# Attention and gated long convolution on one core: another order of the loads, two gate projections of batch 0 ahead of batch 1's k^T v, and two more output buffers at the end

## The chip, the core and the metric

The kernel runs on one core of a Trainium2 chip. The metric is device time in microseconds (us). Before the change the median of three runs is 268.35 us (268.27 to 268.37).

## What is computed

Linear attention without a softmax, normalised per head, feeds a gated convolution over the sequence. Cut to what matters, with B = 8 batches, H = 8 heads, S = 576 positions, D = 64, and 512 channels:

```python
kv  = einsum('bhsd,bhse->bhde', k, v)
o   = einsum('bhsd,bhde->bhse', q, kv)
x   = o / sqrt(mean(o * o, -1) + 1e-6) * g_norm      # then heads side by side: (B, S, 512)
x1, x2, x3 = split(x @ w_proj, 3, axis=-1)
c   = irfft(rfft(x2, axis=1) * rfft(filter_fft, axis=0), n=S, axis=1)
out = (x1 * c * x3) @ w_out
```

Inputs and output are float32.

## The kernel before, in words

**Layout.** Channels lie on the partitions, four tiles of 128 channels (NDC), with the 576 positions in the free dimension. All eight batches are unrolled. For each batch the stages are: `kv` (line 195), k^T v per head, 40 small matmuls (line 204) that accumulate over five chunks of the sequence, four full ones and a tail of 64 rows padded with zeros, and a copy into the diagonal blocks of `kvblk` (line 208); `qtr` (line 210), q transposed by TensorE (line 219) and copied by VectorE (line 222); `att_o`, `att_r`, `att_x` (lines 226 to 261), q times k^T v, its square (line 234), the sum of squares by a matmul with 0/1 blocks (line 250), log and exp for 1/sqrt (lines 251 and 254), and x; `fold` (line 263), which adds and subtracts thirds of the sequence so that the transform becomes three smaller ones; `proj2` (lines 326, 330, 338), the projection x2 that the filter is applied to, on the folded x; `fft` (line 342), the forward transform as matmuls (lines 353, 360), multiplied with the filter's transform on VectorE (lines 355, 356, 361) and summed on GpSimd (line 357); `proj13` (line 363), for one channel tile the projections x1 (copied by ScalarE, line 376) and x3 (multiplied with x1 by VectorE, line 378), sixteen matmuls on line 372; `invc` and `inv`, the inverse transform and the gate; `outp`, the product with w_out and the store. The last batch has a combined end, `last` (line 441), with five output copies (lines 470 and 472), each followed by two stores (line 475), one on SP's queue and one on ScalarE's.

**Once per call.** The cosine and sine tables are made on VectorE and ScalarE (lines 136 to 151) and transposed (`tables`, line 180). The filter is loaded by eight DMAs on SP's queue (`load_filter`, line 115), 1920 KB in all, folded by VectorE (`fold_filter`, line 282) and transformed by TensorE (`gen_h`, line 298).

**Loads.** q, k, v and the weights are cast from float32 to bfloat16 by their DMAs, all on GpSimd's queue: per batch two for k, two for v (`load_kv`, line 81) and two for q (`load_q`, line 89), into two sets of buffers. Their order at the start is k, v, q of batch 0, the parts 1, 0, 2 of w_proj (w2, w1, w3), w_out, and k, v, q of batch 1. At most eight of these transfers are under way: the ninth waits for the first, and so on. GpSimd's queue is in order, and GpSimd's sums of line 357 stand in it too.

**Order of the work.** The kernel is written in a framework that plans each engine's order at build time. Among the instructions whose operands the plan takes as ready, it takes the one that stands first in the program; so an instruction can be put ahead of earlier ones that the plan holds to be waiting. `tc.keep_in_program_order(ins)` pins an instruction behind the one that stands just before it in the program on the same engine. On the chip every engine then runs its planned order and waits on semaphores. PSUM is used as four buffers of two banks (tag `ps`), the output tiles have three buffers (tag `ot`), and the products of `fft` and the two filter tiles `fa` and `fc` share two larger ones (tag `tpw`). The program order before is `kv(0)`, `qtr(0)`, the filter loads, `tables`, the attention of batch 0, `zeros(1)` (the zero rows of batch 1's tails and of its `kvblk`), `fold_filter`, and then for every batch `proj2(b)`, `kv(b + 1)`, `qtr(b + 1)`, for batch 0 `gen_h`, the loads of batch b + 2, and a loop over channel tiles with `fft`, `att_o(b + 1)`, `proj13(b)` and the rest of the attention of b + 1.

Of the kernel before, what the change touches and what calls it, by code (L numbers as in the profile page):

```python
# [9 lines left out]
FP32 = mybir.dt.float32  # L10
# [10 lines left out]
def kernel(  # L21
# [59 lines left out]
    def load_kv(b):  # L81
        for i, src in enumerate((k, v)):
            nc.gpsimd.dma_start(  # L83
                out=kvm[b % 2][i].rearrange("p h c d -> p h (c d)"),
                in_=bass.AP(tensor=src.tensor, offset=src.offset + b * H * S * D,
                            ap=[[4 * D, P], [S * D, H], [1, 4 * D]]))
            nc.gpsimd.dma_start(out=kvt[b % 2][i][:TAIL], in_=src[b, :, 4 * P:S, :].transpose([1, 0, 2]))

    def load_q(b):
        for g in range(2):  # L90
            nc.gpsimd.dma_start(
                out=qb[b % 2][64 * g:64 * g + 64].rearrange("p h (m x) -> p (h m) x", m=3),
                in_=bass.AP(tensor=q.tensor, offset=q.offset + (b * H + 4 * g) * S * D,
                            ap=[[3 * D, 64], [SB * D, 12], [1, 3 * D]]))

    load_kv(0)
    load_q(0)

    wo = consts.tile([P, NDC, DM], BF16)
    wp = consts.tile([P, NDC, D3], BF16)  # L100
# [1 line left out]
    def load_w(dst, src):  # L102
        nc.gpsimd.dma_start(out=dst, in_=src.rearrange("(c p) d -> p c d", p=P))

    for part in (1, 0, 2):
        load_w(wp[:, :, part * DM:(part + 1) * DM], moe_w_proj[:, part * DM:(part + 1) * DM])
    load_w(wo, moe_w_out)
    load_kv(1)
    load_q(1)


    fa = work.tile([P, 4, DM], FP32, name="fa", tag="tpw", bufs=2)
# [2 lines left out]
    def load_filter():  # L115

        for t in (fa, fc):
            tc.keep_in_program_order(nc.vector.memset(t[:, :, 0:1], 0.0))
        f4 = moe_filter_fft.rearrange("(m p c) d -> c p m d", m=3, c=3)
        lo, hi = slice(0, 64), slice(64, 128)  # L120
        for o, i in ((fa[lo, 0:3], f4[0]), (fa[hi, 0:3], f4[1]), (fa[lo, 3], f4[2][:, 1]), (fc[lo, 0], f4[2][:, 0]),
                     (fc[lo, 1], f4[2][:, 2]), (fc[hi, 0:2], f4[0][:, 1:3]), (fc[lo, 2:4], f4[1][:, 1:3]),
                     (fc[hi, 2:4], f4[2][:, 1:3])):
            nc.sync.dma_start(out=o, in_=i)
# [44 lines left out]
    def zeros(i):  # L169
        for t in kvt[i]:  # L170
            tc.keep_in_program_order(nc.vector.memset(t[TAIL:P], 0.0))
        tc.keep_in_program_order(nc.vector.memset(kvblk[i], 0.0))
# [21 lines left out]

    def kv(b):
        (km, vm), (kt, vt) = kvm[b % 2], kvt[b % 2]
        st[b] = {}
        kvp = ps_tile("ps_kv")
        for j in range(NDC):
            for c in range(NSC):  # L200
                for hp in range(2):
                    h = 2 * j + hp
                    kk, vv = (km[:, h, c], vm[:, h, c]) if c < 4 else (kt[:, h], vt[:, h])
                    nc.tensor.matmul(kvp[64 * hp:64 * hp + 64, 0, j * D:(j + 1) * D], kk, vv,  # L204
                                     start=(c == 0), stop=(c == NSC - 1))
        for h in range(2):
            r = slice(64 * h, 64 * h + 64)
            nc.scalar.copy(out=kvblk[b % 2][r, :, r], in_=kvp[r, 0, 0:4 * D].rearrange("p (j e) -> p j e", j=4))

    def qtr(b):  # L210

        qT = work.tile([P, NDC, NR, 64], BF16, name="qT", tag="qT")
        st[b]['qT'] = qT.rearrange("p j c t -> p j (c t)")
        for jj in range(2):
            tp = psp.tile([P, 2, 1024], BF16, name="ps_qT", tag="ps")
            for bank, cs in ((0, range(0, 4)), (1, range(4, NR))):
                for i, c in enumerate(cs):
                    for hp in range(2):
                        nc.tensor.transpose(tp[64 * hp:64 * hp + 64, bank, i * P:(i + 1) * P],  # L219
                                            qb[b % 2][:, 2 * jj + hp, c * D:(c + 1) * D], ident)  # L220
                n = len(cs)
                nc.vector.tensor_copy(  # L222
                    out=qT[:, 2 * jj:2 * jj + 2, cs[0]:cs[0] + n].rearrange("p g c t -> p c g t"),
                    in_=tp[:, bank, 0:n * P].rearrange("p (c g t) -> p c g t", c=n, g=2))
# [57 lines left out]
    def fold_filter():  # L282
        ff = hst['ff'] = work.tile([P, NSC, DM], BF16, name="ff", tag="ff")
        tc.keep_in_program_order(nc.vector.memset(ff[64:P, 1], 0.0))
        t0 = work.tile([P, 2, DM], FP32, name="t0", tag="ot", bufs=3)
        nc.vector.tensor_add(out=t0[:, 0], in0=fa[:, 0], in1=fa[:, 1])
        nc.vector.tensor_add(out=ff[:, 0], in0=t0[:, 0], in1=fa[:, 2])
        nc.vector.tensor_add(out=t0[0:64, 1], in0=fc[0:64, 0], in1=fc[0:64, 1])
        nc.vector.tensor_add(out=ff[0:64, 1], in0=t0[0:64, 1], in1=fa[0:64, 3])
        nc.vector.tensor_sub(out=ff[:, 2], in0=fa[:, 0], in1=fa[:, 2])  # L290
        fc2 = fc.rearrange("p (a b) d -> p a b d", a=2)
        nc.vector.tensor_sub(out=ff[:, 3:5], in0=fc2[:, :, 0], in1=fc2[:, :, 1])
        asc = hst['asc'] = consts.tile([P, 2], FP32, name="asc")
        tc.keep_in_program_order(nc.vector.memset(asc, 2.0 / S))
        tc.keep_in_program_order(nc.vector.memset(asc[0:1, 0:1], 1.0 / S))
        tc.keep_in_program_order(nc.vector.memset(asc[96:97, 0:1], 1.0 / S))
# [144 lines left out]
    def last(b):  # L441

        Y, g13 = st[b]['Y'], st[b]['g13']
        yg = work.tile([P, NDC, S], BF16, name="yg", tag="yg", bufs=3)
        po = [ps_tile("ps_out") for _ in range(3)]

        def part(dc):
            kw = dict(start=(dc == 0), stop=(dc == NDC - 1))
            for c in range(4):
                nc.tensor.matmul(po[c // 2][:, c % 2], yg[:, dc, c * P:(c + 1) * P], wo[:, dc], **kw)  # L450
            for i, y in enumerate((yt[0], yg)):
                nc.tensor.matmul(po[2][64 * i:64 * i + 64, 0], y[:, dc, 4 * P:S], wo[:, dc], **kw)

        for dc in range(NDC):
            ip = ps_tile("ps_inv")
            for g in range(6):
                n = N1 if g < 2 else P
                for h in range(2):
                    nc.tensor.matmul(ip[:, h, 0:TH], Y[:n, g, dc * P:(dc + 1) * P], IV[:n, g, h * TH:(h + 1) * TH],  # L459
                                     start=(g == 0), stop=(g == 5))  # L460
            nc.vector.tensor_mul(out=yg[:, dc].rearrange("p (a b) -> p a b", a=2), in0=ip[:, :, 0:TH],
                                 in1=g13[:, dc].rearrange("p (a b) -> p a b", a=2))
            if dc:
                part(dc - 1)
        part(NDC - 1)
        for c in range(NSC):
            ot = work.tile([P, 2, DM], FP32, name="ot", tag="ot", bufs=3)
            src = po[c // 2][:, c % 2]
            if c % 2:
                nc.vector.tensor_copy(out=ot[:, 0], in_=src)  # L470
            else:
                nc.scalar.copy(out=ot[:, 0], in_=src)
            for i in range(2):
                bb, blk = (b, 2 * c + i) if c < 4 else (b - 1 + i, NR - 1)
                (nc.scalar if i else nc.sync).dma_start(out=o_rows(bb, blk), in_=ot[64 * i:64 * i + 64, 0])


    kv(0)
    qtr(0)
    load_filter()  # L480
    tables()
    for j in range(NDC):
        att_o(0, j)
        if j:
# [4 lines left out]
    att_r(0, NDC - 1)  # L489
    att_x(0, 1)  # L490
    fold(0, 1)
    zeros(1)
    fold_filter()
    for b in range(B):
        nxt = b + 1 < B
        proj2(b)
        if nxt:
            kv(b + 1)
            qtr(b + 1)
        if b == 0:  # L500
            for g in (1, 0, 2):
                gen_h(g)
        if b + 2 < B:
            load_kv(b + 2)
            load_q(b + 2)
        for dc in range(NDC):
            if dc < 3:
                fft(b, (1, 0, 2)[dc])
            if nxt:
                att_o(b + 1, dc)  # L510
            proj13(b, dc)
            if nxt:
                att_r(b + 1, dc)
                if dc % 2:
                    att_x(b + 1, dc // 2)
                    fold(b + 1, dc // 2)
        if b:
            for c0 in (0, 2, 4):
                outp(b - 1, c0)
            del st[b - 1]  # L520
        if not nxt:
            last(b)
            continue
        invc(b)
        inv(b, 0)
        inv(b, 1)
# [30 lines left out]
```

## Time and profile before

| | |
|---|---|
| median of three runs | 268.35 us |
| the profiled execution | 268.72 us |
| its span, first to last instruction | 267.0 us |
| TensorE busy (matmuls) | 223.7 us, 84% |
| VectorE busy | 179.1 us, 67% |
| ScalarE busy | 150.6 us, 56% |
| GpSimd busy | 80.3 us, 30% |
| mean granted TensorE clock | 0.96 |
| read from HBM | 34.47 MB |
| written to HBM | 9.44 MB |

PE is TensorE, DVE VectorE, ACT ScalarE, POOL GpSimd, SP the engine that only issues DMAs; a q behind a name is its queue for issues. Busy time is the time in which an engine executes; a busy share over the whole span is an average over stages that have different limits, so a stage is read by its own stretch of time. A wait is put down to what came last before it ended. "DMA share" is a sum over queues and can exceed 1. Matmuls are pipelined, so their spacing tells more than the duration of one.

### The profile page before, as it was taken

What the parts mean: (1) busy time and instruction counts of PE and PEld (TensorE: products, weight loads), DVE (VectorE), ACT (ScalarE), POOL (GpSimd) and SP (SyncE); (2) the same over time, 40 slices, a digit from 0 to 9 for tenths busy, and PEclk for the clock granted to TensorE, in tenths of its full rate; (3) what the DMA queues carried; (4) which work ended last, traced back from release to release, by engine and by line L of the source; (5) the groups of instructions that cost most, each with busy time, mean ns of one, the idle gap of its engine ahead of it and who ended that gap; (6) DMA issues with size and microseconds to landing.
All of it is one profiled execution on the core that took longest, in us unless ns stands there. A gap on an engine that the chain in (4) does not pass through costs nothing.

```text
span 267.0 us, 4694 instructions
## 1 busy us (share of the span) xinstructions
PE 223.7 (84%) x1895; PEld 137.4 (51%) x1925; DVE 179.1 (67%) x283; ACT 150.6 (56%) x220; POOL 80.3 (30%) x80
## 2 busy tenths in 40 slices
PE   0065309999999999999999999999999999999960
PEld 0052004477466656654665567556654765476630
DVE  6728460295986788577767885778688857786321
ACT  1949104589459745973597459735964596311110
POOL 8742122472076008500760085002400330042000
PEclk9999556999999999999999999999999999999996
DMA  4999999997099059905990599150005001500615
GB/s 50 171 203 238 234 197 193 192 113 85 2 100 169 1 160 118 150 20 177 106 165 5 152 123 145 28 172 2 0 13 147 2 0 29 171 0 0 160 51 147
DMA packets 46296, 27.97 MB, mean 105 GB/s; under 512 B 22274, under 2 KB 40706, under 8 KB 46274
## 3 DMA queue, kind: packets, MB, share of 16 engines
q0 software_dynamic: 39744, 16.26, 50.4%
q1 hardware_dynamic: 6130, 10.75, 15.0%
q10 hardware_dynamic: 400, 0.66, 0.7%
q8 instruction: 15, 0.25, 0.4%
q14 instruction: 7, 0.06, 0.1%
HBM read 34.47 MB, written 9.44 MB: 164 GB/s over the span
## 4 chain that ended last, share of the span: by engine, by line
PE 71%; DMA 13%; ACT 6%; DVE 4%; POOL 2%; issue 2%; ACTq 0%; POOLq 0%
PE ps_x L372 21%; DMA vm<-in_v_dram 9%; PE ps_out L423 9%; PE ps_X L353 6%; PE ps_x L338 6%; PE ps_inv L397 6%; DMA qb<-in_q_dram 3%; PE ps_qT L219 3%; PE ps_inv L459 2%; PE ps_x L326 2%; PE ps_o L233 2%; PE ps_r L250 2%; PE ps_X L360 2%; ACT osb L239 2%; PE ps_kv L204 2%
## 5 line engine op out<-in xcount | busy, mean ns | idle before, releaser
L372 PE MATMUL ps_x<-x,wp 128*128 128x288 bf16 x512 | 67.9, 286 | 0.9
L357 POOL TENSOR_TENSOR Y<-tpw 128x1024 bf16<-128x1024 f32 (+1 forms) x16 | 37.8, 2361 | 74.7 <-DVE tpw L356 74.7
L372 PEld LDWEIGHTS <-wp 128*128 128x128 bf16 x512 | 50.0, 98 | 15.5 <-issue 2.4
L378 DVE TENSOR_TENSOR g<-ps_x,x 128x576 bf16<-128x576 f32 x32 | 24.1, 752 | 14.3 <-ACT x L376 13.0
L234 ACT ACTIVATE sq<-ps_o 128x576 bf16<-128x576 f32 x32 | 20.7, 651 | 18.8 <-PE ps_o L233 18.8
L332 ACT CAST x<-ps_x 128x1024 bf16<-128x1024 f32 x8 | 8.1, 1012 | 37.9 <-PE ps_x L330 37.9
L222 DVE COPY qT<-ps_qT 128x512 bf16<-128x512 bf16 (+1 forms) x32 | 13.4, 454 | 22.6 <-PE ps_qT L219 22.5
L83 POOL DMA_DIRECT2D km<-in_k_dram x8 | 7.4, 925 | 68.3 <-PE ps_qT L219 64.5
L251 ACT ACTIVATE lr<-ps_r,bias_eps 128x576 f32<-128x576 f32 x32 | 23.7, 745 | 6.5 <-PE ps_r L250 5.5
L204 PE MATMUL ps_kv<-vm,km 128*64 128x64 bf16 x256 | 7.2, 204 | 23.6 <-DMA vm<-in_v_dram 23.1
L355 DVE TENSOR_TENSOR tpw<-ps_X,HH 128x1024 f32<-128x1024 f32 (+1 forms) x16 | 19.6, 1224 | 9.4 <-PE ps_X L353 9.4
L423 PE MATMUL ps_out<-wo,yg 128*128 128x512 bf16 x106 | 25.0, 379 | 0.3
L376 ACT CAST x<-ps_x 128x576 bf16<-128x576 f32 x32 | 20.8, 649 | 7.5 <-PE ps_x L372 7.5
L338 PE MATMUL ps_x<-wp,ab 128*128 128x512 bf16 x90 | 23.8, 403 | 0.8 <-DVE ab L273 0.4
L239 ACT ACTIVATE osb<-ps_o,g_col 128x576 bf16<-128x576 f32 x28 | 20.9, 745 | 0.0
L204 PEld LDWEIGHTS <-km 128*64 128x64 bf16 x256 | 6.2, 119 | 26.4 <-issue 18.0
L356 DVE TENSOR_TENSOR tpw<-ps_X,HH 128x1024 f32<-128x1024 f32 (+1 forms) x16 | 19.4, 1215 | 0.0
L397 PE MATMUL ps_inv<-IV,Y 128*128 128x384 bf16 x112 | 19.4, 326 | 0.0
L261 DVE TENSOR_TENSOR x<-osb,rstd 128x1152 bf16<-128x1152 bf16 x16 | 12.1, 756 | 10.2 <-PE ps_x L372 9.9
L254 ACT ACTIVATE rstd<-lr 128x1152 bf16<-128x1152 f32 x16 | 18.6, 1165 | 0.5
L353 PE MATMUL ps_X<-x,FW 128*128 128x512 bf16 (+1 forms) x58 | 17.7, 381 | 0.2 <-ACT x L340 0.2
L402 DVE TENSOR_TENSOR u<-ps_inv,cs 128x768 bf16<-128x768 f32 x14 | 13.4, 954 | 6.2 <-PE ps_inv L397 6.2
(141 smaller groups left out, 358.4 us busy)
## 6 DMA issues: line engine op xcount, KB each, us to landing
out_dram<-ot SPq DMA_DIRECT2D x28, 256.0 KB, 3.8
qb<-in_q_dram POOLq DMA_DIRECT2D x16, 288.0 KB, 8.4
km<-in_k_dram POOLq DMA_DIRECT2D x8, 512.0 KB, 6.1
vm<-in_v_dram POOLq DMA_DIRECT2D x8, 512.0 KB, 8.6
wp<-in_moe_w_proj_dram POOLq DMA_DIRECT2D x3, 512.0 KB, 12.3
out_dram<-ot SPq DMA_DIRECT2D x11, 128.0 KB, 2.9
fa<-in_moe_filter_fft_dram SPq DMA_DIRECT2D x2, 384.0 KB, 9.3
fc<-in_moe_filter_fft_dram SPq DMA_DIRECT2D x3, 256.0 KB, 11.3
```

Of the source, the lines that this page charges most:

```text
L234: nc.scalar.activation(out=s['sq'][:, j].rearrange("p (a b) -> p a b", a=2), in_=op[:, :, 0:TH], func=AF.Square)
L239: nc.scalar.activation(out=o_, in_=op[:, :, 0:TH], func=AF.Copy, scale=g_col)
L251: nc.scalar.activation(out=s['lr'][:, j % 2].rearrange("p (a b) -> p a b", a=2), in_=r2[:, :, 0:TH], func=AF.Ln, scale=1.0 / D, bias=bias_eps)
L338: nc.tensor.matmul(pp[:, cc], ab[:, j, (c0 + cc) * P:(c0 + cc + 1) * P], wp[:, j, DM:2 * DM], start=(j == 0), stop=(j == NDC - 1))
L353: nc.tensor.matmul(xp[:n, ri], FWr[:, ri, 0:n] if c == 1 else FW[:, a, 2 * g + ri, 0:n], x2[:, c], start=(a == 0), stop=(a == len(ks) - 1))
L355: nc.vector.tensor_mul(out=t_[:n, 0], in0=xp[:n], in1=HH[:n, g, 1:3])
L357: nc.gpsimd.tensor_add(out=Y[:n, 2 * g:2 * g + 2], in0=t_[:n, :, 0], in1=t_[:n, :, 1])
L372: nc.tensor.matmul(pp[:, h, 0:TH], w_, x[:, j, h * TH:(h + 1) * TH], start=(j == 0), stop=(j == NDC - 1))
L376: nc.scalar.copy(out=x1, in_=pp[:, :, 0:TH])
L378: nc.vector.tensor_mul(out=st[b]['g13'][:, dc].rearrange("p (a b) -> p a b", a=2), in0=pp[:, :, 0:TH], in1=x1)
L397: nc.tensor.matmul(ip[:, i, 0:2 * SB], Y[:, g, d_], IV[:, g, 0:2 * SB], start=(g == 2), stop=(g == 5))
L423: nc.tensor.matmul(pp[:, cc], yg[:, dc, c * P:(c + 1) * P], wo[:, dc], start=(dc == 0), stop=(dc == NDC - 1))
```

## The change

Nothing in the computation changes. Six edits, all in order or buffers:

- q of batch 0 is loaded ahead of k and v, and w_out behind the loads of batch 1.
- `load_filter` and `qtr(0)` come ahead of `kv(0)`; `tables` comes behind the attention and fold of batch 0.
- `fold_filter`, the gate projections `proj13(0, 0)` and `proj13(0, 1)`, and `zeros(1)` come between `proj2(0)` and `kv(1)`; the matmuls of `kv(1)` are pinned in program order. The loop later skips the two.
- `gen_h(1)` and `gen_h(0)` come ahead of `qtr(1)`, `gen_h(2)` behind it.
- The copies of k^T v of batch 0 go from ScalarE to VectorE. The six operations of `fold_filter` are pinned, the differences first.
- In `last`, the fourth and fifth output tile take the larger buffers of the tag `tpw`.

```diff
+    load_q(0)
     load_kv(0)
-    load_q(0)
...
     for part in (1, 0, 2):
         load_w(wp[:, :, part * DM:(part + 1) * DM], moe_w_proj[:, part * DM:(part + 1) * DM])
-    load_w(wo, moe_w_out)
     load_kv(1)
     load_q(1)
+    load_w(wo, moe_w_out)
...
-                    nc.tensor.matmul(kvp[64 * hp:64 * hp + 64, 0, j * D:(j + 1) * D], kk, vv,
-                                     start=(c == 0), stop=(c == NSC - 1))
+                    mm = nc.tensor.matmul(kvp[64 * hp:64 * hp + 64, 0, j * D:(j + 1) * D], kk, vv,
+                                          start=(c == 0), stop=(c == NSC - 1))
+                    if b == 1:
+                        tc.keep_in_program_order(mm)
...
+            if b == 0:
+                nc.vector.tensor_copy(out=o_, in_=i_)
+            else:
+                nc.scalar.copy(out=o_, in_=i_)
...
+        pin = tc.keep_in_program_order
+        pin(nc.vector.tensor_sub(out=ff[:, 2], in0=fa[:, 0], in1=fa[:, 2]))
+        pin(nc.vector.tensor_sub(out=ff[:, 3:5], in0=fc2[:, :, 0], in1=fc2[:, :, 1]))
+        pin(nc.vector.tensor_add(out=t0[:, 0], in0=fa[:, 0], in1=fa[:, 1]))
...
-            ot = work.tile([P, 2, DM], FP32, name="ot", tag="ot", bufs=3)
+            ot = work.tile([P, 2, DM], FP32, name="ot", tag="ot", bufs=3) if c < 3 else \
+                work.tile([P, 2, 2, DM], FP32, name="ot_", tag="tpw", bufs=2)[:, 0]
...
+    load_filter()
+    qtr(0)
     kv(0)
-    qtr(0)
-    load_filter()
-    tables()
...
     fold(0, 1)
-    zeros(1)
-    fold_filter()
+    tables()
     for b in range(B):
         nxt = b + 1 < B
         proj2(b)
+        if b == 0:
+            fold_filter()
+            proj13(0, 0)
+            proj13(0, 1)
+            zeros(1)
         if nxt:
             kv(b + 1)
+        if b == 0:
+            gen_h(1)
+            gen_h(0)
+        if nxt:
             qtr(b + 1)
         if b == 0:
-            for g in (1, 0, 2):
-                gen_h(g)
+            gen_h(2)
...
-            proj13(b, dc)
+            if b or dc >= 2:
+                proj13(b, dc)
```

## Rows read from the trace of the kernel before

**Rows 1.** The page's busy tenths in 40 slices of 6.7 us.

```profile
PE   0065309999999999999999999999999999999960
...
DMA  4999999997099059905990599150005001500615
```

**Rows 2.** Waits of TensorE, 20 to 75 us: total, times, longest in us.

```profile
PE ps_kv L204 <- DMA vm<-in_v_dram: 10.6, 1, 10.6
```

**Rows 3.** Windows: length, then each engine's busy us (count), PEclk, DMA share, GB/s.

```profile
30.10:40.10 10.00, 0.00 (x0) 0.03 (x1) 7.17 (x15) 0.00 (x0) 1.85 (x3) 0.50 1.45 210
40.10:45.20 5.10, 5.10 (x24) 1.56 (x24) 0.00 (x0) 1.36 (x2) 1.49 (x2) 0.59 1.58 192
45.20:66.90 21.70, 20.92 (x200) 13.91 (x202) 12.13 (x19) 18.02 (x30) 9.34 (x8) 1.00 1.15 135
```

**Rows 4.** Timeline, TensorE: start, duration, line, operation, tiles, count, wait before.

```profile
16.57 1.07 PE L219 MATMUL ps_qT<-ident,qb 128*64 128x128 bf16 x16 [2.13 <-DMA qb<-in_q_dram]
...
27.57 1.91 PE L338 MATMUL ps_x<-wp,ab 128*128 128x512 bf16 x4 [0.20 <-issue]
...
40.10 0.43 PE L204 MATMUL ps_kv<-vm,km 128*64 128x64 bf16 x8 [10.62 <-DMA vm<-in_v_dram]
...
45.67 0.20 PE L204 MATMUL ps_kv<-vt,kt 128*64 128x64 bf16 x2
...
53.01 2.12 PE L372 MATMUL ps_x<-x,wp 128*128 128x288 bf16 x16
```

**Rows 5.** Transfers issued at 15 to 16 us: count, size, us from issue to landing.

```profile
vm<-in_v_dram POOLq DMA_DIRECT2D x1, 512.0 KB, 24.9
```

**Rows 6.** DMA packets of 13-14, 22-23, 28-30 us; q0 is GpSimd's queue, q1 SP's.

```profile
q0 software_dynamic: 510, 0.19, 160.0%
...
DMA packets 213, 0.20 MB, mean 204 GB/s; under 512 B 14, under 2 KB 213, under 8 KB 213
...
q0 software_dynamic: 213, 0.20, 123.6%
...
q1 hardware_dynamic: 216, 0.35, 82.7%
q0 software_dynamic: 217, 0.11, 40.6%
```

**Rows 7.** Timeline, VectorE and SP's queue, around the filter loads.

```profile
11.71 0.27 DVE L172 MEMSET kvblk<- 128x256 uint32 x1
...
19.97 1.98 SPq L124 DMA_DIRECT2D fa<-in_moe_filter_fft_dram  x3
...
30.72 0.69 DVE L286 TENSOR_TENSOR t<-fa 128x512 f32<-128x512 f32 x1 [3.80 <-DMA fa<-in_moe_filter_fft_dram]
```

**Rows 8.** Timeline, ScalarE, attention of batch 0 and of batch 1.

```profile
26.43 1.16 ACT L254 ACTIVATE rstd<-lr 128x1152 bf16<-128x1152 f32 x1
...
46.23 0.75 ACT L208 CAST kvblk<-ps_kv 64x256 bf16<-64x256 f32 x2
...
49.75 0.69 ACT L309 ACTIVATE HH<-ps_h,asc 128x512 f32<-128x512 f32 x1 [2.76 <-PE ps_h L307]
...
65.71 1.16 ACT L254 ACTIVATE rstd<-lr 128x1152 bf16<-128x1152 f32 x1
```

**Rows 9.** Costliest groups: count, busy us, mean ns of one, idle before.

```profile
L378 DVE TENSOR_TENSOR g<-ps_x,x 128x576 bf16<-128x576 f32 x32 | 24.1, 752 | 14.3 <-ACT x L376 13.0
...
L376 ACT CAST x<-ps_x 128x576 bf16<-128x576 f32 x32 | 20.8, 649 | 7.5 <-PE ps_x L372 7.5
```

**Rows 10.** Timeline, the output copies and ScalarE's DMA issues (ACTq) at the end.

```profile
257.93 1.40 ACTq L475 DMA_DIRECT2D out_dram<-ot  x2
...
260.06 1.83 ACTq L475 DMA_DIRECT2D out_dram<-ot  x2
260.67 0.69 DVE L470 COPY ot<-ps_out 128x512 f32<-128x512 f32 x1 [2.05 <-DMA out_dram<-ot]
262.07 0.58 ACT L472 COPY ot<-ps_out 128x512 f32<-128x512 f32 x1 [2.04 <-DMA out_dram<-ot]
```

More of the change, by code (lines that the diff above doesn't have):

```diff
@@ L196, in kv @@
         (km, vm), (kt, vt) = kvm[b % 2], kvt[b % 2]
-        st[b] = {}
+        st.setdefault(b, {})
         kvp = ps_tile("ps_kv")
@@ L203, in kv @@
                     kk, vv = (km[:, h, c], vm[:, h, c]) if c < 4 else (kt[:, h], vt[:, h])
-                    nc.tensor.matmul(kvp[64 * hp:64 * hp + 64, 0, j * D:(j + 1) * D], kk, vv,
-                                     start=(c == 0), stop=(c == NSC - 1))
+                    mm = nc.tensor.matmul(kvp[64 * hp:64 * hp + 64, 0, j * D:(j + 1) * D], kk, vv,
+                                          start=(c == 0), stop=(c == NSC - 1))
+                    if b == 1:
+                        tc.keep_in_program_order(mm)
         for h in range(2):
             r = slice(64 * h, 64 * h + 64)
-            nc.scalar.copy(out=kvblk[b % 2][r, :, r], in_=kvp[r, 0, 0:4 * D].rearrange("p (j e) -> p j e", j=4))
+            o_, i_ = kvblk[b % 2][r, :, r], kvp[r, 0, 0:4 * D].rearrange("p (j e) -> p j e", j=4)
+            if b == 0:
+                nc.vector.tensor_copy(out=o_, in_=i_)
+            else:
+                nc.scalar.copy(out=o_, in_=i_)
     def qtr(b):
         qT = work.tile([P, NDC, NR, 64], BF16, name="qT", tag="qT")
-        st[b]['qT'] = qT.rearrange("p j c t -> p j (c t)")
+        st.setdefault(b, {})["qT"] = qT.rearrange("p j c t -> p j (c t)")
         for jj in range(2):
@@ L285, in fold_filter @@
         t0 = work.tile([P, 2, DM], FP32, name="t0", tag="ot", bufs=3)
[L286 to L290, printed above, removed]
-        fc2 = fc.rearrange("p (a b) d -> p a b d", a=2)
-        nc.vector.tensor_sub(out=ff[:, 3:5], in0=fc2[:, :, 0], in1=fc2[:, :, 1])
+        fc2 = fc.rearrange("p (a b) d -> p a b d", a=2)
+        pin = tc.keep_in_program_order
+        pin(nc.vector.tensor_sub(out=ff[:, 2], in0=fa[:, 0], in1=fa[:, 2]))
+        pin(nc.vector.tensor_sub(out=ff[:, 3:5], in0=fc2[:, :, 0], in1=fc2[:, :, 1]))
+        pin(nc.vector.tensor_add(out=t0[:, 0], in0=fa[:, 0], in1=fa[:, 1]))
+        pin(nc.vector.tensor_add(out=ff[:, 0], in0=t0[:, 0], in1=fa[:, 2]))
+        pin(nc.vector.tensor_add(out=t0[0:64, 1], in0=fc[0:64, 0], in1=fc[0:64, 1]))
+        pin(nc.vector.tensor_add(out=ff[0:64, 1], in0=t0[0:64, 1], in1=fa[0:64, 3]))
         asc = hst['asc'] = consts.tile([P, 2], FP32, name="asc")
```

## Prediction, made before the changed kernel ran

> **What bounds the kernel now.** I begin with the busy tenths of the page [rows 1]. TensorE shows 9 in every slice from the seventh on, so from 40 us to nearly the end of the last batch it is the bound, and there only less TensorE work could help; this change removes none. The hole is at the front: the fifth slice shows 3 and the sixth 0, while the DMA engines stand at 9 from the second slice to the ninth. So I ask who ended that hole. The waits of TensorE have one long entry: line 204, k^T v of batch 1, waited 10.6 us for v of batch 1 [rows 2]. The windows give its size and its after-effect [rows 3]: from 30.1 to 40.1 us no matmul at all, and the granted clock is 0.50 there and 0.59 in the 5.1 us after it (the lower level, 1.2 GHz, most of that time), then 1.00. The timeline of TensorE shows how it came about [rows 4]: matmuls of the filter projection of batch 0 (line 338, four in 1.91 us), then at 40.10 us eight matmuls of batch 1's k^T v, then the rest of the projection, and the last of k^T v at 45.67. TensorE takes its instructions in order, so a load of the next batch held up work of this one.
>
> **The change, part by part.**
>
> *The awaited load.* k^T v of batch 1 is now pinned behind the second gate projection, so it no longer stands inside the filter projection. When does its v land? It took 24.9 us from its issue [rows 5] and ended the wait at 40.1 [rows 4], so it landed at 40.0. One load fewer stands ahead of it: w_out's 512 KB, at the 204 GB/s of a stretch in which the GpSimd queue was alone [rows 6], is 2.6 us. That gives 37.4. All other bytes ahead of it are the same, whatever their order, so this sum holds even where single loads shift. The 64 KB tail of v follows it within 1 us.
>
> *The front.* q comes first, so its transposes finish early, and v gates k^T v of batch 0 instead. The last of q, k and v was used at 16.57 [rows 4], and that bytewise end stays. But the filter loads move on SP's queue: their issue, at 19.97, followed a memset pinned behind the q copies; now that memset is pinned behind the first zeros, which end at 12.0, so SP issues at about 12.1 [rows 7], in the middle of q, k and v. Where both queues are active they alternate packet for packet (216 against 217 in 2 us), and GpSimd's queue falls from 510 small packets a us to 108 [rows 6]. The eight filter transfers are 1920 KB in 2 KB rows, 960 packets. They began late: in the window 22 to 23, over 2 us after the issue, all 213 packets were GpSimd's [rows 6]. With 4 us of delay they begin when v has landed: cost 0. With 1 us they begin at 13.1, when about 2 us of small packets (1000 at 510 a us) are left, which then take 9.3 us: cost 7. I take 1 us, near the late start that the rows show, and keep the rest for a rival. The Trainium skill, DMA: Bandwidth & Descriptors, section "Issuing engines are not separate DMA queues", says that transfers started by different engines run on the same 16 DMA engines and interleave; this rule speaks against moving the filter ahead, and by it alone v would come near the cost of 7. The rows agree on the interleaving, not on its start.
>
> After that the attention of batch 0 is a chain of ScalarE and VectorE as before. The copies of k^T v go from ScalarE (0.75 for the two [rows 8]) to VectorE, where no row has this shape: bounded by a 0.27 memset of 256 columns and a 0.69 operation on 512 [rows 7] for each, 0.2 less to 0.6 more for the pair; I take 0, as 0.37 lies between. The table copies leave this stretch of VectorE; a filter operation or two (0.69) may slip in. So the filter projection starts at about 28 instead of 27. Its second half waited behind the filter's first sum on VectorE, which itself waited 3.8 us for its load [rows 7]. Now x and the fold stand ahead of it: the last 1/sqrt ended at 27.6 [rows 8], and with 1 us for v and 2 for x and fold the second half can start at 30.6. It filled the 40.5 to 45.2 between the two parts of k^T v, with the clock low at first [rows 3, 4]; the same 4.7 us give 35.3.
>
> *The early gate projections.* Sixteen matmuls of line 372 (one channel tile) take 2.0 us at the full clock [rows 4], two tiles 4.0: TensorE is at 39.3. At the lower clock all the way it would be 43.3. Their weights (two more loads of 2.6 us behind w2, doubled by the filter) are due by about 30: no wait. VectorE's filter sums, seven operations or some 5 us at 0.69 each, now lie beside this in a stretch of 8, and GpSimd has only issues: cost 0; without that cover the filter transforms would start 1 to 2 us later.
>
> *k^T v of batch 1.* v is there from 37.4, so no wait. But its zero rows are now set by VectorE after the second gate product (0.75 [rows 9]) by two memsets of 0.27 [rows 7]: the first tail matmul waits until about 40.6, with eight matmuls ahead of it. Queued behind on TensorE are the rest of k^T v and, in program order, the filter transforms. With 0.8 us for the rest, k^T v ends at 41.4, where it ended at 45.9: 4.5 us earlier, and 4.0 us of gate projections are already done.
>
> *The rest of batch 0.* Here ScalarE takes over. From its k^T v copy (end 46.98) to the last 1/sqrt (66.87) it needed 19.9 us, with one wait of 2.76 us for the filter transform [rows 8] and 18.0 us busy in 21.7 [rows 3]. That transform now follows k^T v directly, 6 matmuls or 1.4 us at half the spacing of line 338 [rows 4], so some 0.4 of the wait is left: 2.3 less. Two copies of line 376 (0.65 each [rows 9]) are done earlier: 1.3 less. Starting from 42.3, 16.3 us give 58.6 instead of 66.9: a lead of 8.3. TensorE was busy 20.9 us there [rows 3]; without 4.0 for the gates and 0.8 for k^T v it needs 16.1, to 57.5. The two nearly tie, and they feed each other, so I take off 0.5. **Front: 7.8 us.** From there the batches follow as before, bound by TensorE, and the lead is kept: q of batch 1 follows v with 576 KB, 2.9 us at 204 GB/s, so it lands at 41.3, and its transposes come after the transforms at about 43, and batch 2 has until 65. w_out, now behind q, is first needed after batch 1's gate projections: cost 0. GpSimd's DMA issues each wait for an older load to land; its first sum of Y stands behind some of them, and Y is needed only for the inverse, so cost 0.
>
> *The end.* The fourth output copy (VectorE, 260.67) and the fifth (ScalarE, 262.07) each waited 2.0 us for an output buffer [rows 10]. With a free one the fourth goes at once. The fifth still stands behind two DMA issues on ScalarE's queue that begin at 260.06 and took 1.83 us with the fourth's wait in them; the pair before took 1.40 [rows 10]. So it starts at 261.5 instead of 262.07, or up to 0.5 sooner where the pair's own waits go too: gain 0.7.
>
> **The sum**: 7.8 + 0.7 = 8.5 us. The profiled execution took 268.72 (its span 267.0 and 1.7 around it): 260.2. The median shown is 0.37 below that execution, so I predict **259.9 us**.
>
> **The rivals.**
>
> *The filter starves v of batch 0.* Filter packets start within 1 to 2 us, v lands 4 to 7 us late, and the whole front of batch 0 moves by what exceeds my 1 us, 3 to 6. For: the alternation in the rows. Against: no filter packet for over 2 us. The lead is 8.5 - 3 to 8.5 - 6: 262.9 to 265.9 us. Here the skill's interleaving rule would be right at once.
>
> *The wait moves to q of batch 1, and the kernel is slower.* Only k^T v is pinned. The order is planned at build time by what the planner takes as landed, and in the kernel before it put batch 1's first eight matmuls into the gap of the filter projection on a load that came 10 us later. It can do this with the transposes of q of batch 1, which need no zeros. Then TensorE stops until 41.3, runs 36 transposes at the lower clock (16 took 1.07 [rows 4], so 2.4), 4.7 of projection, 4.0 of gates and 2.1 of k^T v with its zeros: 54.5, 8.6 later than before. The 3.6 us saved on ScalarE and the 0.7 at the end leave 4.3: 272.7 us. It decides as soon as one transpose stands before the projection's second half. Against: q came after v in the same queue, and before they were not hoisted.
>
> *TensorE stays at the lower clock.* If the gaps at 28 to 31 keep the clock at 0.5 into the gate projections, these cost 4.0 more, ScalarE starts later: 264. Against: dense work from 40.1 on brought 1.00 by 45.2 [rows 3].
>
> *It does not come to bear*: another load, or k^T v's new zeros, holds TensorE to 45 as before, and only the end's 0.7 is left: 267.7.
>
> **How the numbers follow.** Forecast 0.60 (alone 257.5 to 262.0: 2.4 less if the transforms fill the zeros' wait, the tie costs nothing and v is 0.5 early; 2.1 more if v, the filter operations and the copies each take their upper ends), filter before v 0.20, lower clock 0.06, q of batch 1 0.08, nothing comes to bear 0.06 (half of it within the bound). The range runs from 257.3 to 265.2: it takes in the forecast, the lower clock and most of the first rival, and leaves out under 0.2. A measurement of this kernel can tell 0.2% (0.5 us) from no change. Faster 0.88, same 0.04, slower 0.08.
>
> **What would show it.** Right: TensorE's 10.6 us wait on line 204 is gone or below 2 us, line 372 stands before line 204 of batch 1, k^T v of batch 1 ends near 41.4, v of batch 1 lands near 37, ScalarE's last 1/sqrt of batch 1 ends near 58.6, and the windows after it have the old length. Wrong: filter packets before 14 us and k^T v of batch 0 after 20 (first rival); a wait of line 219 on q of batch 1 until about 41 us (second); clock 0.5 in the gate projections (third).

## The result, and the profile after

The changed kernel took **258.37 us** (median of four runs, 257.95 to 261.74) against 268.36 for the kernel before on the same chip: a ratio of 0.9666, 95% interval 0.9589 to 0.9742. Run again, unchanged, it took 258.20 against 268.74, ratio 0.9616 (0.9596 to 0.9635). It is faster, by 10.0 to 10.5 us by the medians, where 8.5 were forecast. The ratios are of means, and the first takes in two more executions, of 261.59 and 258.66 us: by the mean of those six, 259.45, the gain is 9.0, by the mean of the second four 10.3. The run first profiled was the 261.74 one (span 260.0); the second profile is of a run of 257.88 (span 256.1). Both are read here, because one step of the prediction is part of what sets them apart.

The page's busy tenths in the first profile, in slices of 6.5 us:

```profile
PE   0237899769999999999999999999999999999970
...
PEclk9999799997999999999999999999999999999997
DMA  4999999992493549353984297420023002400515
```

The waits of TensorE, 20 to 75 us (total, times, longest; Y is the product of the two transforms, which GpSimd sums and the inverse transform reads):

```profile
PE ps_r L256 <- ACT sq L240: 2.3, 4, 0.7
PE ps_c L392 <- POOL Y L364: 2.1, 1, 2.1
```

Windows of the stretches of [rows 3], and a new one:

```profile
30.10:40.10 10.00, 9.95 (x88) 5.61 (x89) 6.62 (x14) 4.66 (x7) 4.62 (x6) 0.94 1.55 194
40.10:45.20 5.10, 4.65 (x73) 2.75 (x67) 1.64 (x4) 3.98 (x8) 1.57 (x2) 1.00 1.50 196
...
58.70:62.10 3.40, 3.40 (x12) 1.60 (x11) 3.40 (x8) 0.15 (x1) 0.00 (x0) 0.50 0.40 49
```

The hole is filled: TensorE, idle for all of 30.1 to 40.1 before, is busy 9.95 of these 10 us, and the wait of [rows 2] is gone from the list. The timeline of TensorE shows the new order (the old lines 326, 338, 372 and 307 are now 333, 345, 379 and 314):

```profile
27.27 0.39 PE L333 MATMUL ps_x<-wp,rr 128*128 128x512 bf16 x1 [0.68 <-DVE rr L278]
...
29.72 1.17 PE L379 MATMUL ps_x<-x,wp 128*128 128x288 bf16 x4
30.68 0.63 PE L345 MATMUL ps_x<-wp,ab 128*128 128x512 bf16 x1
...
33.86 3.59 PE L379 MATMUL ps_x<-x,wp 128*128 128x288 bf16 x28
37.38 0.32 PE L204 MATMUL ps_kv<-vm,km 128*64 128x64 bf16 x8
37.63 1.69 PE L314 MATMUL ps_h<-ff,FW 128*128 128x512 bf16 x6
...
39.67 0.22 PE L204 MATMUL ps_kv<-vt,kt 128*64 128x64 bf16 x2
...
40.17 0.20 PE L204 MATMUL ps_kv<-vt,kt 128*64 128x64 bf16 x2
```

The gates (line 379) stand ahead of batch 1's k^T v, whose first eight matmuls find v landed; the filter transforms fill the wait for its new zeros.

**Where some of it went again.** The last 1/sqrt of batch 1 ends at 57.05, 9.8 us sooner than in [rows 8], yet batch 2's k^T v begins at 66.34 where it began at 72.81 before: the lead has shrunk to 6.5. Rows of ScalarE and TensorE, then GpSimd's timeline in this profile:

```profile
55.89 1.16 ACT L260 ACTIVATE rstd<-lr 128x1152 bf16<-128x1152 f32 x1
...
66.34 0.32 PE L204 MATMUL ps_kv<-vm,km 128*64 128x64 bf16 x8
```

```profile
47.49 0.88 POOL L83 DMA_DIRECT2D vm<-in_v_dram  x1 [3.51 <-DMA km<-in_k_dram]
48.37 0.69 POOL L87 DMA_DIRECT2D vt<-in_v_dram  x1
50.97 1.49 POOL L91 DMA_DIRECT2D qb<-in_q_dram  x2 [1.91 <-PE ps_x L379]
52.46 4.66 POOL L364 TENSOR_TENSOR Y<-tpw 128x1024 bf16<-128x1024 f32 x2
```

The two sums of Y of batch 0 had their products from VectorE by 47.8 and 50.0, but stand behind the loads of batch 3, two of which wait in these rows (3.51 and 1.91 us), and begin at 52.46. VectorE and TensorE then show, in this profile:

```profile
54.87 2.88 DVE L267 TENSOR_TENSOR x<-osb,rstd 128x1152 bf16<-128x1152 bf16 x1 [1.42 <-PE ps_x L379]
...
57.19 0.83 PE L392 MATMUL ps_c<-IV,Y 97*128 97x192 bf16 x8 [2.11 <-POOL Y L364]
57.86 4.44 PE L404 MATMUL ps_inv<-IV,Y 128*128 128x384 bf16 x16
```

TensorE waits 2.1 us for Y, and 1.5 us after it has begun again its granted clock is 0.50 for 3.4 us (the window above), the lower level of 1.2 GHz: the inverse takes 4.44 us. In the second profile the same places read:

```profile
49.86 4.67 POOL L364 TENSOR_TENSOR Y<-tpw 128x1024 bf16<-128x1024 f32 x2
...
53.42 1.73 DVE L267 TENSOR_TENSOR x<-osb,rstd 128x1152 bf16<-128x1152 bf16 x1 [1.42 <-PE ps_x L379]
...
54.58 0.83 PE L392 MATMUL ps_c<-IV,Y 97*128 97x192 bf16 x8 [0.96 <-POOL Y L364]
55.25 2.77 PE L404 MATMUL ps_inv<-IV,Y 128*128 128x384 bf16 x16
```

The sums are late there too, but by 1.0, the clock stays at 1.00 and the inverse takes 2.77. The rest of what parts the two profiles is at the front, where v of batch 0 is first used at 16.29 and at 14.80: of the 3.8 us between the starts of batch 2's k^T v (66.34 and 62.50), 1.5 come from there and 2.3 from Y and the clock.

### The profile page after: what moved, and what is told of

Read it like the earlier page. It is cut to its first block, busy times and chain, and to the rows that moved or that the text cites. A ratio compares the mean times of both kernels' runs of the same rounds, so it can differ in the third digit from the quotient of the medians.

```text
span 260.0 us, 4691 instructions
## 1 busy us (share of the span) xinstructions
PE 225.3 (87%) x1895; PEld 138.7 (53%) x1925; DVE 181.2 (70%) x285; ACT 150.1 (58%) x218; POOL 80.5 (31%) x80
## 4 chain that ended last, share of the span: by engine, by line
PE 72%; DMA 12%; ACT 6%; POOL 5%; issue 2%; DVE 1%; ACTq 1%; POOLq 0%; DVEq 0%
PE ps_x L379 20%; PE ps_out L430 9%; PE ps_inv L404 8%; DMA qb<-in_q_dram 7%; PE ps_X L360 7%; PE ps_x L345 7%; DMA wp<-in_moe_w_proj_dram 5%; PE ps_qT L225 3%; PE ps_inv L466 2%; PE ps_x L333 2%; PE ps_r L256 2%; PE ps_o L239 2%; PE ps_c L392 2%; ACT sq L240 2%; PE ps_X L367 2%; PE ps_kv L204 2%
## 5 line engine op out<-in xcount | busy, mean ns | idle before, releaser
L345 PE MATMUL ps_x<-wp,ab 128*128 128x512 bf16 x90 | 22.9, 394 | 0.2
L225 PE MATMUL ps_qT<-ident,qb 128*64 128x128 bf16 x288 | 12.2, 232 | 11.4 <-DMA qb<-in_q_dram 10.5
L267 DVE TENSOR_TENSOR x<-osb,rstd 128x1152 bf16<-128x1152 bf16 x16 | 14.2, 886 | 9.9 <-PE ps_x L379 9.9
L404 PE MATMUL ps_inv<-IV,Y 128*128 128x384 bf16 x112 | 21.0, 345 | 0.0
L430 PEld LDWEIGHTS <-yg 128*128 128x128 bf16 x112 | 10.9, 98 | 11.9
```

The source lines that it names most:

```text
L345: nc.tensor.matmul(pp[:, cc], ab[:, j, (c0 + cc) * P:(c0 + cc + 1) * P], wp[:, j, DM:2 * DM], start=(j == 0), stop=(j == NDC - 1))
L404: nc.tensor.matmul(ip[:, i, 0:2 * SB], Y[:, g, d_], IV[:, g, 0:2 * SB], start=(g == 2), stop=(g == 5))
L430: nc.tensor.matmul(pp[:, cc], yg[:, dc, c * P:(c + 1) * P], wo[:, dc], start=(dc == 0), stop=(dc == NDC - 1))
```

## Experiments

A stage is placed by two starts in TensorE's timeline: of k^T v of batch 0 (v has landed) and of batch 2 (the front is over). From the latter to the end of the span all kernels with the old end need 194.2 us, those with the new one 193.6 to 193.7, and the last one of the table 194.0. For the run with transforms in the gaps the profile is of its longest execution (260.65), which stands 2.4 us above the next one: there v's tail came late, and TensorE waited 2.37 us for it amid batch 0's k^T v. The median in the table is of its other five, and its starts are left out.

| kernel | median us (runs) | ratio to before, 95% | k^T v of batch 0 | of batch 2 |
|---|---|---|---|---|
| before | 268.36 (4) | | 12.49 | 72.81 |
| after | 258.37 (4) | 0.9666 (0.9589 to 0.9742) | 16.29 | 66.34 |
| after again | 258.20 (4) | 0.9616 (0.9596 to 0.9635) | 14.80 | 62.50 |
| Y ahead of batch 3's loads | 258.24 (6) | 0.9614 (0.9585 to 0.9644) | 15.92 | 63.01 |
| before, k^T v pinned | 267.82 (10) | 0.9973 (0.9956 to 0.9989) | 13.13 | 71.59 |
| before, pinned, early gates | 263.55 (4) | 0.9808 (0.9793 to 0.9823) | 12.22 | 67.20 |
| before, new end alone | 268.01 (12) | 0.9977 (0.9950 to 1.0004) | 13.09 | 72.60 |
| after, w_out ahead | 260.79 (4) | 0.9707 (0.9681 to 0.9732) | 15.30 | 65.42 |
| after, filter late | 260.40 (4) | 0.9686 (0.9664 to 0.9708) | 15.48 | 64.94 |
| after, filter first | 263.01 (4) | 0.9778 (0.9752 to 0.9805) | 21.51 | 68.56 |
| Y ahead, two copies moved | 258.44 (6) | 0.9611 (0.9581 to 0.9642) | 15.21 | 62.32 |
| and two more | 257.48 (6) | 0.9573 (0.9540 to 0.9606) | 14.86 | 61.38 |
| and transforms in the gaps | 257.08 (5) | 0.9559 (0.9521 to 0.9597) | | |
| and another end | 257.64 (5) | 0.9605 (0.9579 to 0.9631) | 16.09 | 62.58 |

**One part at a time, on the kernel before.** First the pin alone, then the early gates with it.

```
-  nc.tensor.matmul(kvp..., kk, vv, ...)
+  mm = nc.tensor.matmul(kvp..., kk, vv, ...)
+  if b == 1: tc.keep_in_program_order(mm)
```

> Before, with the matmuls of batch 1's k^T v held in program order, and nothing else: they can't stand inside the filter projection of batch 0 any more, the order of loads, the zeros and the gates stay. Theory A (the hole was one of order: TensorE held up by a load of the next batch): the 10.6 us wait inside the projection goes, but w_out is still ahead of batch 1's v, which comes at 40, and TensorE has only the projection (some 6 us) to fill the time; k^T v of batch 1 starts at 40 and ends at about 43 to 44 instead of 45.9: 2 to 3 us gained, 265.5 to 266.5. Theory B (the order of loads is what matters, and TensorE waits for v to 40 either way): under 1 us, 267.5 to 268.4.

The pin moved batch 1's k^T v as meant: it ended at 40.96, 4.9 us sooner than in [rows 4]. But the kernel gained 0.9 us, as theory B had it. The waits of TensorE, 20 to 75 us, with the pin alone:

```profile
PE ps_x L340 <- DVE ab L275: 4.6, 2, 4.2
PE ps_x L328 <- DVE rr L274: 2.6, 1, 2.6
PE ps_qT L221 <- DMA qb<-in_q_dram: 2.4, 1, 2.4
PE ps_kv L204 <- DMA vm<-in_v_dram: 1.5, 1, 1.5
```

The 2.6 for line 328 was there before, under its old number. In place of the 10.6 stand three waits of 8.1 in all, for the fold (4.2), q and v. The projection's second half now waits for a fold that stands on VectorE behind the filter's first sum, which waits for its load until 30.59; then TensorE has nothing to run until v and q of batch 1 come at 39.8 and 43.4. All four gate tiles are still to be done after that.

```
+  if b == 0: proj13(0, 0); proj13(0, 1)
   if nxt: kv(b + 1)
...
-  proj13(b, dc)
+  if b or dc >= 2: proj13(b, dc)
```

> Before, with k^T v of batch 1 held in program order and two channel tiles of batch 0's gate projections ahead of it; the loads stay in the old order, with the filter issued at 20 us. Theory A (the early gates are what fills the wait for v, and the order of the loads gives 2.6 us more): k^T v of batch 1 starts at 40 with 4 us of gates already done, 6 to 7 us gained in all: 261.5 to 263, so the loads' order and the rest are worth the 3 to 4 us that are left to after. Theory B (the order of loads carries most): 265 or more.

4.3 us more, all else as before: work put into the hole is what gained. It lies between the theories, nearer A: order and gates carry 5.2 of the 10.5 us, and 5.3 are left for the loads and the end.

**One part undone, on the changed kernel.** w_out back ahead of batch 1's k, v and q:

```
+  load_w(wo, moe_w_out)
   load_kv(1); load_q(1)
-  load_w(wo, moe_w_out)
```

> After, with w_out's 512 KB back ahead of k, v and q of batch 1. Theory A (v and q of batch 1 are what is awaited at 36 to 42 us): v of batch 1 lands 2.6 us later, near 40, q near 43, k^T v ends near 41 to 42 and the transposes stop TensorE until 43: 1 to 2.6 us above after, 259.3 to 261. Theory B (the early gates and the filter transforms cover it): within 0.5 us of after.

```profile
40.04 0.32 PE L204 MATMUL ps_kv<-vm,km 128*64 128x64 bf16 x8 [3.08 <-DMA vm<-in_v_dram]
```

2.6 us slower, theory A: in this kernel's timeline of TensorE v of batch 1 is awaited to 40.04.

The filter's loads back behind q and k^T v of batch 0 (issued at 18.34 instead of 11.62):

```
-  load_filter(); qtr(0); kv(0)
+  qtr(0); kv(0); load_filter()
```

> After, with the filter's two memsets and eight loads moved behind q's transposes and k^T v of batch 0, as they were before: SP issues them near 18 us instead of 12. Theory A (the early issue is worth something: the filter sums on VectorE then wait for their loads and stand ahead of the fold or of the filter transforms, as in the kernel with k^T v pinned alone): k^T v of batch 1 or the transforms move 2 to 4 us later, 260 to 262. Theory B (filter packets begin only when v of batch 0 has landed, whenever they are issued): within 0.5 us of after, 257.7 to 258.7.

2.2 us slower, theory A. VectorE's timeline in this kernel has five of the six filter sums behind the first gate product, starting at 35.40 to 39.49 (29.56 to 32.74 where the filter is early), and the memsets of batch 1's zeros among and behind them:

```profile
35.40 1.22 DVE L295 TENSOR_TENSOR ff<-fc 128x1024 bf16<-128x1024 f32 x1
...
40.31 0.27 DVE L171 MEMSET vt<- 64x256 uint32 x1
```

On TensorE the rest of the transforms and the tail of k^T v, which need these, stand in this kernel behind the first transposes of batch 1's q, which wait for their load:

```profile
41.25 0.41 PE L225 MATMUL ps_qT<-ident,qb 128*64 128x128 bf16 x8 [1.67 <-DMA qb<-in_q_dram]
```

TensorE ends batch 1's k^T v at 43.1 instead of 39.3. How much of this is the late sums and zeros (ready by 40.6) and how much the wait for q that the new order brought with it is not shown. The parts add up: 0.9 (pin) + 4.3 (gates) + 2.6 (order of loads) + 2.2 (filter early) + 0.6 (end, below) = 10.6, against 10.5 measured. Two are added to the kernel before and two are taken from the changed one, and each is known to a few tenths at best, so that the sum agrees this closely is in part luck. The load of q ahead of k and v, the later tables, the order of the filter transforms and the copies on VectorE were not tried alone.

**Can the filter starve v?** The filter's loads issued first of all:

```
+  load_filter()
   nc.vector.tensor_copy(out=kcol, in_=ki)
...
-  load_filter()
```

> After, with the two memsets and the eight filter loads on SP's queue issued at the very start, ahead of everything else on VectorE and SP, so that they are active beside q, k and v of batch 0 from the first microseconds. Theory A (the rival of the prediction: two active queues alternate packet for packet, so the filter's 960 packets hold up the small packets of q, k and v): v of batch 0 is used 5 to 9 us later than the 16.0 us of after (14.8 to 16.3 in the profiles), the lead falls by as much: 263 to 267. Theory B (the queue with the small packets keeps its rate, the filter fills what it leaves): v within 1 us of after, 258 to 259.

Theory A. SP's issues began at 1.52, v of batch 0 came at 21.51, and the kernel took 4.8 us more. DMA packets in the windows 8 to 9 and 13 to 14 us of this kernel, and in 13 to 14, 15 to 16 and 16 to 17 us of after's second profile (q0 is GpSimd's queue, q1 SP's; packets, MB, share):

```profile
q0 software_dynamic: 273, 0.10, 86.2%
q1 hardware_dynamic: 58, 0.10, 51.0%
...
q1 hardware_dynamic: 111, 0.21, 88.7%
q0 software_dynamic: 109, 0.04, 34.4%
```

```profile
q0 software_dynamic: 547, 0.19, 162.3%
...
q0 software_dynamic: 185, 0.19, 113.2%
q1 hardware_dynamic: 20, 0.04, 12.0%
...
q0 software_dynamic: 93, 0.10, 55.8%
q1 hardware_dynamic: 92, 0.19, 55.2%
```

With both active the small packets fall from 547 a us to 273, and in each us from 9 to 14 to 99 to 136, beside 95 to 112 of SP's. GpSimd's packets also began later: its first load was issued at 2.47 and moved at 6.2, where in after's second profile it was issued at 2.45 and moved at 4.0; so some 2 of the 6.7 us by which v is late are a later start. The Trainium skill, DMA: Bandwidth & Descriptors, section "Issuing engines are not separate DMA queues", says that transfers interleave whichever engine started them; these rows agree. In after the filter does no harm because SP's first packets move only in the window 15 to 16, four us after the issue at 11.62, when v has landed.

**The late sums of Y.** All six loads of batch 3 held in program order, so that GpSimd sums first:

```
-  load_kv(b + 2); load_q(b + 2)
+  load_kv(b + 2, b == 1); load_q(b + 2, b == 1)   (pinned if the last argument is true)
```

> The changed kernel once more, unchanged, for a second profile. Its times so far lie in two groups, four from 257.95 to 258.66 us and two at 261.59 and 261.74, and the profile seen is of the second group. Theory A (GpSimd's first sums of Y stand behind the loads of batch 3, the inverse waits for them until 57.2 us, and in the pause TensorE's granted clock falls for the next 3.4 us): both groups come again, and a profile of the first group shows the same late sums but no, or a shorter, low clock after them; its last 1/sqrt of batch 1 then still ends near 57, and its output of batch 0 comes some 3 us sooner than in the other. Theory B (the 3 us come from the loads at the front, which land differently from run to run): a profile of the first group shows k^T v of batch 1 ended 3 us or so earlier than the 40.4 us seen, or the stretch up to 40 us otherwise ordered.

> After, with the six loads of batch 3 held in program order, so that on GpSimd's queue the sums of Y of batch 0 stand ahead of them. Theory A (late sums of Y cost the time lost between 55 and 62 us): TensorE's wait of 2.1 us for Y goes, VectorE's operation that took 2.9 us beside the second sum no longer meets it at that point, the clock stays at 1.00, and no run is above 259: median 256.3 to 257.0, 1.4 to 2.0 us below after. Theory B (the sums are hidden and the loads decide): no difference within 0.5 us, or slower, since batch 3's loads start some 5 us later.

Of the unchanged kernel's four runs none was above 259.33, so only one of its two groups came again; the second profile has the sums late with the clock at 1.00, as A said, and the last 1/sqrt at 55.60. It also has the front 1.5 us earlier, which B said. Both hold a part. With the sums first, GpSimd's and VectorE's timelines read:

```profile
47.97 4.68 POOL L368 TENSOR_TENSOR Y<-tpw 128x1024 bf16<-128x1024 f32 x2 [8.21 <-DVE tpw L367]
...
54.91 0.76 DVE L271 TENSOR_TENSOR x<-osb,rstd 128x1152 bf16<-128x1152 bf16 x1 [1.42 <-PE ps_x L383]
```

TensorE's wait for Y is gone and the clock is 1.00 throughout; the lead at the last 1/sqrt (57.09 against 66.87, 9.8) is kept to batch 2's k^T v (9.8), where after lost 3.3 and 1.0 of it. Yet the median is the same, and one run took 260.03: this is A's mechanism without A's gain. From k^T v of batch 0 to that of batch 2 the edit saves 0.6 us (47.09 against 47.70), while the arrival of v moves by 1.5 us from run to run. That the late sums make the runs near 261.7 is therefore seen in one profile and not shown: the execution of 260.65 named above has the sums first and is long by v's late tail, as theory B would have it, and the mean granted clock does not part the groups (0.981 and 0.977 in the two long runs, 0.974 in those of 257.95 and 258.66).

**What is late next.** On top of the sums first, two copies of the filter transforms go from ScalarE to VectorE, then two scaled copies of batch 1's attention, then the transforms of batch 0 move between matmuls that waited for ScalarE's squares.

```
-  nc.scalar.activation(out=HH[:n, g, 2], in_=hp[:n, 1], func=AF.Copy, scale=-2.0 / S)
+  nc.vector.tensor_scalar_mul(out=HH[:n, g, 2], in0=hp[:n, 1], scalar1=-2.0 / S)
```

> After with Y's sums ahead of batch 3's loads (as in the run before with that edit), and two of ScalarE's seven copies of the filter transforms, 0.6 us each, done by VectorE, which has over 2 us free between 40 and 45 us. Theory A (from k^T v of batch 1 to the last 1/sqrt of batch 1, about 40 to 57 us, ScalarE sets the end): 1.0 to 1.3 us below the run without it, 256.9 to 257.3, the last 1/sqrt near 55. Theory B (TensorE, or the sums of Y, set the end there): under 0.4 us.

No gain, theory B: the two starts stay 47.11 apart. ScalarE waits 1.26 and 0.62 us for TensorE just behind these copies, so it doesn't set the end there. The comparison is not clean, though: in this trace the granted clock is 0.50 in 25 to 30 us, where it is 1.00 in the one compared with, and that one waits 1.0 us for q of batch 1, so a gain of some tenths could be hidden.

```
-  if b == 0:
+  if b == 0 or (b == 1 and j >= 2):
       nc.vector.tensor_scalar_mul(out=o_, in0=op[:, :, 0:TH], scalar1=g_col)
```

> The run with two copies of the filter transforms on VectorE, and now also two of ScalarE's four scaled copies of batch 1's attention (0.75 us each, channel tiles 2 and 3) on VectorE, which is idle 1.5 us at 50.5 and 1.4 at 52.8. Theory A (from 45 to 56 us, where ScalarE is busy without a gap, ScalarE alone sets the end): 1.2 to 1.5 us faster, 256.7 to 257.2. Theory B (TensorE is dense from 48 to 57.7 too, the two tie, and its two waits of 0.74 us at 45 to 48 stay): under 0.5 us.

Between the theories: 0.6 us by the trace (46.52 apart), 257.48 by the median, the six runs from 256.75 to 258.05. VectorE takes 0.82 for what took ScalarE 0.75.

```
-  if dc < 3: fft(b, (1, 0, 2)[dc])
+  if dc < 3 and (b or dc == 0): fft(b, (1, 0, 2)[dc])
...
+  if b == 0 and dc < 2: fft(b, dc * 2)      (behind att_o, ahead of att_r)
```

> The kernel of the run before, with the transforms of batch 0's low bins and middle bins put between the two matmuls pairs of batch 1's attention that TensorE waited between (0.74 us twice, for ScalarE's squares). Theory A (TensorE and ScalarE tie from 45 to 57 us, so both have to be relieved): 1.0 to 1.8 us below after, 256.5 to 257.3, and the two waits gone. Theory B (something else, the sums of Y or VectorE's gates, is late next): no gain over the kernel before it.

By the trace theory B: TensorE's wait for the squares fell from 2.0 to 0.8 us in all and the starts are 46.49 apart (both read in the next kernel, whose front is the same), 0.03 less than without. By the times it is open: 257.08 lies 1.1 below the 258.20 of after, in A's range, but 0.4 below the kernel before it, with intervals that overlap. This kernel, the one before it and the one after it have lower medians than after, by 0.6 to 1.1 us; their intervals overlap with its.

**The end.**

```
-  ot = work.tile([P, 2, DM], FP32, name="ot", tag="ot", bufs=3)
+  ot = ... if c < 3 else work.tile([P, 2, 2, DM], FP32, name="ot_", tag="tpw", bufs=2)[:, 0]
```

> Before, with the fourth and fifth output copies of the last batch in buffers of their own and nothing else changed. Theory A (the prediction's end term): 0.5 to 0.7 us below before, 268.0 to 268.2; the fourth copy no longer waits, the fifth starts 0.5 or so sooner. Theory B (the fifth copy stands behind ScalarE's DMA issues all the same): under 0.2 us.

By the medians 0.85 us, by the means 0.6, with an interval that just includes none; by the trace the stretch from the first output copy to the end is 9.1 us (257.12 to 266.2) where it was 9.7 (257.32 to 267.0): 0.6, theory A. But the copies did not go as A said. ScalarE, VectorE and ScalarE's queue at the end of this kernel:

```profile
257.73 1.40 ACTq L476 DMA_DIRECT2D out_dram<-ot  x2
...
259.25 0.58 ACT L473 COPY ot<-ps_out 128x512 f32<-128x512 f32 x1 [1.55 <-DVE ot L471]
...
259.94 0.69 DVE L471 COPY ot__3125<-ps_out 128x512 f32<-128x512 f32 x1 [1.51 <-ACT ot L473]
```

The fourth copy still waits 1.51 us, now for the third, which stands behind ScalarE's two issues. So the last kernel issued all copies ahead of all output transfers and spread these over SP (six), ScalarE (three) and GpSimd (one):

```
-  (nc.scalar if i else nc.sync).dma_start(...)      (behind each copy)
+  qs[i].dma_start(...)                              (behind all five copies)
```

> The kernel of the run before (the two transforms between the attention's matmuls, copies moved to VectorE), with the last batch's five output copies issued before any of their ten output loads, and those spread so that ScalarE issues three behind its last copy, GpSimd one and SP six. Theory A (at the end ScalarE's copies stand behind its own output issues: with the buffers free, the third copy began 1.55 us after the first had ended, and the fifth 1.5 us after the third): the fifth copy ends near 1.9 us after the first began instead of 4.8, SP's last issue about 1.5 us sooner: 1.3 to 1.8 us faster than the run before, 255.6 to 256.2. Theory B (the issues' own time and the landing of the last transfer set the end): under 0.5 us.

```profile
247.13 1.07 ACT L485 COPY ot<-ps_out 128x512 f32<-128x512 f32 x2 [9.23 <-PE ps_out L461]
...
247.74 3.01 SPq L491 DMA_DIRECT2D out_dram<-ot  x4
...
248.35 0.68 DVE L483 COPY ot__3119<-ps_out 128x512 f32<-128x512 f32 x1
...
250.84 0.95 SPq L491 DMA_DIRECT2D out_dram<-ot__3119  x1
251.89 0.91 SPq L491 DMA_DIRECT2D out_dram<-ot__3121  x1
```

Theory B. The copies ended 1.9 us after the first began, as A asked, and nothing came of it: SP's six issues took 0.75 to 0.95 us each, where its single ones took 0.47 in the run with the new end alone, the last ended 5.7 us after the first copy began, and the end took 9.5 us.

## Why the prediction was right, and where it was not

The direction, the mechanism and the range held. By the medians the sum was 1.5 us short, by the mean of the first six runs 0.5. Three terms were off, in both directions, so that it came as close as this is in part luck.

*The awaited load*: right. w_out was taken at 2.6 us and its place is worth 2.6; v is awaited to 40.04 with it ahead, and found at 37.38 and even 36.30 without.

*The front*: the filter was issued at 12.36 and 11.62 (12.1 forecast), but the cost of 1 us for filter packets beside v was wrong, it was 0: the delay from issue to packets was four us. It was a choice between 0 and 7, near the end for which [rows 6] spoke (none of SP's packets over 2 us after an issue), and that row was right. The filter projection began at 27.27 and 25.84 (28), its second half at 30.68 and 29.79 (30.6).

*Second half and gates*: the 4.7 us came from a stretch at the lower clock; at a granted clock of 0.94 to 1.00 and with four gate matmuls hoisted, half and gates ended at 37.4 and 36.3, not 39.3. This term was mis-sized by about 2 us.

*k^T v of batch 1 and ScalarE's chain*: its end came at 40.4 and 39.3 (41.4), the last 1/sqrt at 57.05 and 55.60 (58.6): the lengths held (16.7 and 16.3 us, 17.2 forecast), the start was early. The tie of TensorE and ScalarE is not shown: relieving ScalarE gave 0 and 0.6 us by the traces, and relieving TensorE's waits on top of it 0.03, so what sets that end stays open.

*"Y is needed only for the inverse, so cost 0"*: wrong. The lead moved the sums' inputs and the inverse earlier, but GpSimd's load issues wait for older loads to land, and these kept their pace. It cost 1.0 us in one profile and, with the clock that fell behind it, 3.3 in the other. This took back part of what the terms before had been short. With the sums first, 0.6 us returned by the trace and nothing by the median.

*The end*: 0.7 forecast, 0.6 by the trace, with another path: the fourth copy did not go at once.

*The rivals*: the filter starving v is real where its packets start early (263.0, in the range given for it), but there the filter was issued before GpSimd's first load; at 12 us it did no harm. The rate taken for the starved queue, 108 packets a us, was right (99 to 136). The transposes of q of batch 1 were not hoisted. The lower clock did come at the front, but ended before most of the gates: in 25 to 30 us it was 0.80 in after's first profile (1.00 in the second) and 0.50 in the run with two copies moved. It cost little there: the last 1/sqrt of batch 1 came 40.8 us after the start of batch 0's k^T v in both profiles of after, and 41.2 in the run with two copies moved as in the one without.

## What to carry to other kernels

A long wait is worth what other work can be put into it: here moving the waiting instruction away gained 0.9 us of a hole of 10, and putting the gates into it 4.3 more. When a lead is gained, look on every queue for work that stands behind waits which do not move with it: here an engine that is busy for a third of the span took 1 to 3 us of the lead in two profiles, though the median did not show it when that work was moved. And in this kernel issuing the copies at the end sooner gained nothing, since the transfers' own issues followed.

## What was not expected of the hardware

From SP's issue of the filter to its first packets passed four us (11.62, window 15 to 16) while GpSimd's queue was full of packets; issued at 1.52, before GpSimd's first load, the filter was moving at 3.0. In that run it was GpSimd's first load, at 2.47 behind the filter, that took 3.7 us to its first packets (1.5 in after's second profile, with nothing ahead of it).

VectorE's product of two tensors in SBUF, the on-chip memory beside PSUM (line 267), took 2.88 and 1.73 us beside GpSimd's sum and 0.76 without it; both times it ended 0.6 us after the sum. A product with one operand in PSUM (line 385, 52.69 us) ran its 0.76 beside the same sums. The Trainium skill, SBUF — State Buffer, section "SBUF: two separate sides", says that such a VectorE operation and a GpSimd one hold a shared pair of ports for a whole instruction, one after the other; these rows agree.
